# Attention and channel mix on one core: units of 448 tokens across batch ends, scores in 64x64 tiles, TensorE in traced order, weight decode with PSUM, shared staging slots

## The chip, the cores and the metric

The kernel runs on one core of one Trainium2 chip. The metric is the device time of one launch in microseconds (us). TensorE (PE) multiplies, VectorE (DVE), ScalarE (ACT) and GpSimd (POOL) do the elementwise work, and SyncE (SP) issues every DMA of this kernel.

## The reference

Sliding-window attention feeds a channel mix. Attention's arrays are float32, and there are 8 batches, 8 heads, 576 tokens and 64 columns per head.

```python
# attention, per batch and head: window of 64 keys, causal
scores = (q @ k.T) / sqrt(64)
mask = (rel >= 0) & (rel < 64)            # rel = query - key
attn = exp(where(mask, scores, -1e9) - max)
attn = attn / (attn.sum(-1) + 1e-9)
x = heads side by side(attn @ v)          # 576 x 512 for each batch

# channel mix, per batch
x_prev = x shifted down one token, zero first
xk = mu_k * x + (1 - mu_k) * x_prev
xr = mu_r * x + (1 - mu_r) * x_prev
kk = maximum(xk @ w_k, 0.0)               # 512 x 1024
out = sigmoid(xr @ w_r) * ((kk * kk) @ w_v)
```

The weights w_k, w_v and w_r arrive as float64 and are decoded to float32 on the chip, since the arithmetic of the reference is kept to float32 accuracy.

## The kernel before

**Attention.** Two heads fill the 128 partitions, so there are 32 pairs. The 576 queries of a pair are 9 blocks of 64, and three blocks are a group: 96 groups in all. For a group, `scores` issues three matmuls `s` (L149). Their weights are a tile `qbd` that holds a block's queries of both heads with zeros where one head's rows meet the other's columns, so one 128x128 matmul gives the scores of both heads against 128 keys (64 keys in a pair's first block). DVE masks and takes the minimum (`sm`, L152), ACT takes the exponent and its sum (`pr`, L155), DVE inverts the sum (`rs`, L158, L159) and POOL normalises (L161). `flip` transposes the three weights on PE (`t`, L168) and ACT copies them out (`pt`, L170). `mix_v` multiplies with the values for two groups at a time (`x`, L182: 64 columns of weights, so the tile shape on PE is 128x64), and ACT copies the result to `xT` (L187). The three steps of a group are pulled one at a time, each a stage behind the next group's scores.

**Channel mix.** A unit is 288 tokens, half a batch: 16 units. `time_mix` makes `xr` and `xk` (DVE L221 and L224, ACT L225, POOL L226), each split in two float32r parts. Every product takes three matmuls per 128 rows of contraction (`product`, L235: `m`, 128x128 weights, 288 columns): 48 for `r`, 96 for `k` and 96 for `v`, 240 a unit. Behind a product of `r` come four ACT operations and one of DVE (L247 to L253), behind one of `k` ACT, POOL, ACT, DVE (L262 to L266), behind one of `v` a DVE operation and an output DMA (L275, L276). A product accumulates in one of four PSUM buffers.

**Weight decode.** 20 chunks of 128x512 doubles (512 KB each) come through three staging buffers `wst` (L102). Five DVE operations (L107 to L113) build the float, ACT rounds it to the first float32r part (L116), POOL subtracts for the second (L117). The 20 chunks are pulled while the first batch's attention and the first units are issued.

**What sets the order.** The program pulls generators in an interleaved way: first the whole attention of batch 0 with decode in between, then per step of a unit (20 steps of 12 matmuls) one attention step and at the start one decode chunk. The instructions are then put in order on each engine by a scheduler that works with a simulated timeline, and it may move instructions of every engine, PE included, past each other as far as the data allow.

Of the kernel before, what the change touches and what calls it, by code (L numbers as in the profile page):

```python
# [23 lines left out]
NG = NB // G  # L24
# [6 lines left out]
STAGES = 3 * (NP * NG + 2)   # steps of a batch's attention  # L31
LEAD = 8             # steps by which attention is ahead of the channel mix
MIX_AT = 11          # step of a MoE unit at which the next one's mixing begins
R_BUFS = 4           # gates, which become outputs
WB = 3               # chunks of weights in flight
WC = 512             # weight columns decoded at a time
# High words of doubles as float32 values: 2**-127, and the largest float32 of 12 bits.
# [5 lines left out]
def attn_rwkv_kernel(ctx, tc, qT, kT, v2, mu_k, mu_r, w_k, w_v, w_r, out):  # L43
# [12 lines left out]
    # queries of a pair by block, the heads' apart: zero where a head's rows meet the  # L56
    # other head's columns
    qbd = [const.tile([P, NB, 2, W], F32, name=f"qbd{i}") for i in range(2)]
    nc.vector.memset(qbd[0][:, :G], 0.0)
    nc.vector.memset(qbd[0][:, G:], 0.0)  # L60
# [7 lines left out]
    mask0 = const.tile([P, W], F32, name="mask0")  # L68
    nc.gpsimd.memset(mask, 0.0)
    nc.gpsimd.memset(mask0, 0.0)  # L70
    for h in range(2):
        m = mask[h * W:(h + 1) * W]
        nc.gpsimd.affine_select(out=m, in_=m, compare_op=ALU.is_ge, fill=NEG, base=-1,
                                pattern=[[1, P]], channel_multiplier=-1)
        nc.gpsimd.affine_select(out=m, in_=m, compare_op=ALU.is_ge, fill=NEG, base=W,
                                pattern=[[-1, P]], channel_multiplier=1)
        m = mask0[h * W:(h + 1) * W]
        nc.gpsimd.affine_select(out=m, in_=m, compare_op=ALU.is_ge, fill=NEG, base=0,
                                pattern=[[-1, W]], channel_multiplier=1)

    nc.gpsimd.memset(qbd[1], 0.0)
    # the first group's weights: its first block has none for the other keys
    pr0 = const.tile([P, G, P], F32, name="pr0")
    nc.gpsimd.memset(pr0[:, 0, W:], 0.0)
# [9 lines left out]
    # A weight comes as a double: its low word and its high word. The float's bits are  # L94
    # sign and top exponent bit of the high word, its next 27 bits and 3 bits of the low
    # word; a magnitude outside float32's normal range is brought to its ends first.
    def weights():
        for dst, src in ((wr_s, w_r), (wk_s, w_k), (wv_s, w_v)):
            for c in range(0, dst.shape[3], WC):
                for i in range(dst.shape[2]):  # L100
                    st = tmp.tile([P, WC, 2], U32, name="wst", bufs=WB)
# [3 lines left out]
                    t = tmp.tile([P, WC], U32, name="wt")  # L105
                    tf = t.bitcast(F32)
                    nc.vector.tensor_scalar(t, hi, 0x7FFFFFFF, None, op0=ALU.bitwise_and)  # L107
                    nc.vector.tensor_scalar(tf, tf, HI_MIN, HI_MAX, op0=ALU.max, op1=ALU.min)  # L108
                    nc.vector.tensor_scalar(t, t, 3, 0x3FFFFFF8,  # L109
                                            op0=ALU.logical_shift_left, op1=ALU.bitwise_and)  # L110
                    nc.vector.scalar_tensor_tensor(t, hi, 0xC0000000, t,  # L111
                                                   op0=ALU.bitwise_and, op1=ALU.bitwise_or)
                    nc.vector.scalar_tensor_tensor(t, lo, 29, t,  # L113
# [7 lines left out]
    loaded = {}  # L121

    def load_pair(n, cuts=(0, NB)):
        """cuts: the blocks at which q and k are cut into transfers."""
        q = qbd[n % 2]
        k = ld.tile([P, S], F32, name="k")
        for i0, i1 in zip(cuts, cuts[1:]):
            nc.sync.dma_start(k[:, i0 * W:i1 * W], kT[n, :, i0 * W:i1 * W])
            for h in range(2):
                nc.sync.dma_start(q[h * W:(h + 1) * W, i0:i1, h, :],  # L130
                                  qT[n, h * W:(h + 1) * W, i0 * W:i1 * W].rearrange("p (i r) -> p i r", r=W))
        v = ld.tile([P, 2, 4, P], F32, name="v")
        nc.sync.dma_start(v, v2[n])
        loaded[n] = (q, k, v)

    def scores(n, g):
        q, k, _ = loaded[n]
        ps = ps_s.tile([P, G, P], F32, name="s")
        # sm = -(scaled and masked scores), nmax = their minimum
        sm = at.tile([P, G, P], F32, name="sm", bufs=3)  # L140
        nmax = at.tile([P, G], F32, name="nmax", bufs=4)
        pr = pr0 if g == 0 else at.tile([P, G, P], F32, name="pr")
        sums = at.tile([P, G], F32, name="sums", bufs=4)
        # keys of a block's window: the block before and the own one, if there are two
        nks = [W if g == 0 and j == 0 else P for j in range(G)]
        for j, nk in enumerate(nks):
            i = G * g + j
            k0 = (i + 1) * W - nk
            nc.tensor.matmul(ps[:, j, :nk], q[:, i].rearrange("p h r -> p (h r)"),  # L149
                             k[:, k0:k0 + nk], start=True, stop=True)  # L150
        for j, nk in enumerate(nks):
            nc.vector.tensor_tensor_reduce(sm[:, j, :nk], ps[:, j, :nk], mask if nk == P else mask0,  # L152
                                           scale=-SCALE, scalar=FAR, op0=ALU.add, op1=ALU.min,
                                           accum_out=nmax[:, j:j + 1])
            nc.scalar.activation(pr[:, j, :nk], sm[:, j, :nk], AF.Exp, bias=nmax[:, j:j + 1], scale=-1.0,  # L155
                                 accum_out=sums[:, j:j + 1])
# [3 lines left out]
        for j, nk in enumerate(nks):  # L160
            nc.gpsimd.tensor_scalar(pr[:, j, :nk], pr[:, j, :nk], rs[:, j:j + 1], 1.0,  # L161
                                    op0=ALU.mult, op1=ALU.mult)
        return pr

    def flip(pr):
        ps = ps_t.tile([P, G, P], F32, name="t")
        for j in range(G):
            nc.tensor.transpose(ps[:, j, :], pr[:, j, :], ident)  # L168
        pt = at.tile([P, G, P], F32, name="pt", bufs=3)
        nc.scalar.copy(pt, ps)  # L170
        return pt

    def mix_v(groups, xT):
        """Groups (pair, group, weights) together, as changing to half the columns costs."""
        ps = ps_x.tile([P, len(groups), G, W], F32, name="x")
        for e, (n, g, pt) in enumerate(groups):
            v = loaded[n][2]
            for j in range(G):
                i = G * g + j
# [117 lines left out]
    xTs = {}  # L297
# [69 lines left out]
```

## Time and profile before

| | |
|---|---|
| time, median of 3 runs | 712.29 us (709.93 to 712.74) |
| profiled execution, first to last instruction (span) | 711.3 us; the page gives no other time for it, and the median of the runs is 1.0 us above |
| instructions | 15989 |
| PE busy | 682.2 us (96%), 5856 matmul records |
| DVE, ACT, POOL busy | 415.5, 413.9, 364.9 us |
| HBM read, written | 46.14 MB, 9.44 MB |

A float32 matmul leaves two matmul records (s: 288 matmuls, 576 records; x: 576 and 1152), a float32r matmul (m) and a transpose (t) one. Records overlap, because matmuls are pipelined: the mean length of a record is not the time between two of them. That time is read from the chain of waits, where a piece "PE m L235 x744" has its length and its count. Start times are counted from the first instruction.

### The profile page before, as it was taken

The numbers are of one execution on the slowest core, as the hardware profiler recorded it, in microseconds if no ns is written. First come the engines' busy times: TensorE is split into PE (matmuls) and PEld (weight loads), VectorE is DVE, ScalarE is ACT, GpSimd is POOL, SyncE is SP. The second block draws the span as 40 slices with busy tenths as digits, with TensorE's granted clock in tenths as the row PEclk, the third lists the DMA queues.
The fourth block names the chain that finished last, engine by engine and source line by source line (L and its number), as shares of the span: only waits on it lengthen the run. The fifth ranks groups of instructions, "written<-read, shape, count | busy, mean of one in ns | idle before, by whom it ended". The sixth has DMA issues, their size and how long they took to land.

```text
span 711.3 us, 15989 instructions
## 1 busy us (share of the span) xinstructions
PE 682.2 (96%) x5856; PEld 657.9 (92%) x5856; DVE 415.5 (58%) x1326; ACT 413.9 (58%) x1397; POOL 364.9 (51%) x580
## 2 busy tenths in 40 slices
PE   6878878999999999999999999999999999999998
PEld 5766777799999999999999999999999999999998
DVE  3999999955545455465535455463645556463421
ACT  4768775663626383748566575756756475644351
POOL 4788898754335272554626355453624546252420
PEclk9999898999999999999999999999999999999999
DMA  8885666620000001221222222211323221000000
GB/s 208 237 234 152 189 178 176 166 73 26 10 34 2 34 31 64 65 89 45 85 63 72 68 64 88 73 55 44 95 66 94 67 64 48 18 1 35 26 9 34
DMA packets 59742, 56.61 MB, mean 80 GB/s; under 512 B 40592, under 2 KB 49040, under 8 KB 59664
## 3 DMA queue, kind: packets, MB, share of 16 engines
q1 hardware_dynamic: 59664, 55.59, 26.7%
q8 instruction: 46, 0.75, 0.5%
q14 instruction: 32, 0.26, 0.1%
HBM read 46.14 MB, written 9.44 MB: 78 GB/s over the span
## 4 chain that ended last, share of the span: by engine, by line
PE 80%; DVE 15%; POOL 1%; issue 1%; DMA 1%; SPq 1%; ACT 0%
PE m L235 68%; PE s L149 6%; PE x L182 4%; PE t L168 3%; DVE sm L152 2%; DVE wt L111 2%; DVE wt L107 2%; DVE wt L113 2%; DVE xm L224 1%; DVE wt L109 1%; DVE wt L108 1%; DVE rs L158 1%; POOL pr L161 1%; DMA qbd<-qT 1%; DVE d L221 1%
## 5 line engine op out<-in xcount | busy, mean ns | idle before, releaser
L235 PE MATMUL m<-ks,wv_s 128*128 128x288 f32 x1536 | 226.1, 301 | 1.0 <-ACT wv_s L116 0.9
L235 PE MATMUL m<-xk,wk_s 128*128 128x288 f32 x1536 | 221.2, 299 | 2.0 <-POOL wk_s L117 2.0
L161 POOL TENSOR_SCALAR pr<-pr,rs 128x128 f32<-128x128 f32 (+1 forms) x288 | 129.7, 467 | 173.0 <-DVE rs L159 62.4
L235 PEld LDWEIGHTS m<-ks,wv_s 128*128 128x128 f32 x1536 | 208.7, 190 | 2.5 <-ACT wv_s L116 1.3
L235 PEld LDWEIGHTS m<-xk,wk_s 128*128 128x128 f32 x1536 | 207.0, 189 | 3.6 <-POOL wk_s L117 2.2
L155 ACT ACTIVATE pr<-sm,nmax 128x128 f32<-128x128 f32 (+1 forms) x288 | 111.6, 391 | 68.0 <-DVE nmax L152 67.9
L263 POOL TENSOR_TENSOR kf<-kf 128x288 f32<-128x288 f32 x128 | 93.2, 733 | 81.1 <-ACT kf L262 80.1
L266 DVE TENSOR_TENSOR ks<-kf,ks 128x288 fp32r<-128x288 f32 x128 | 72.6, 571 | 71.5 <-ACT ks L265 71.3
L235 PE MATMUL m<-xr,wr_s 128*128 128x288 f32 x768 | 113.1, 299 | 1.0 <-POOL xr L226 1.0
L235 PEld LDWEIGHTS m<-xr,wr_s 128*128 128x128 f32 x768 | 103.5, 188 | 2.4 <-POOL xr L226 1.9
L149 PE MATMUL s<-k,qbd 128*128 128x128 f32 (+1 forms) x576 | 88.4, 294 | 15.7 <-DVE nmax L152 9.0
L149 PEld LDWEIGHTS s<-k,qbd 128*128 128x128 f32 x576 | 79.0, 205 | 19.0 <-DVE nmax L152 11.2
L226 POOL TENSOR_TENSOR xr<-xm,xr 128x288 fp32r<-128x288 f32 x64 | 56.4, 891 | 71.2 <-ACT xr L225 68.4
L152 DVE CUSTOM_DVE_ANT_0 sm<-s,mask 128x128 f32<-128x128 f32 (+1 forms) x288 | 66.7, 276 | 36.1 <-PE s L149 36.0
L262 ACT ACTIVATE kf<-m 128x288 f32<-128x288 f32 x128 | 52.2, 409 | 36.8 <-PE m L235 29.5
L224 DVE SCALAR_TENSOR_TENSOR xm<-d,muk,xT 128x288 f32<-128x288 f32 x64 | 55.2, 862 | 26.7 <-POOL xr L226 26.6
L265 ACT CAST ks<-kf 128x288 fp32r<-128x288 f32 x128 | 55.1, 431 | 24.9 <-POOL kf L263 24.5
L253 DVE SCALAR_TENSOR_TENSOR r<-th,e 128x288 f32<-128x288 f32 x64 | 34.2, 535 | 50.4 <-ACT th L251 50.1
L247 ACT ACTIVATE e<-m 128x288 f32<-128x288 f32 x64 | 26.2, 410 | 60.9 <-PE m L235 60.7
L168 PE MATMUL t<-ident,pr 128*128 128x128 f32 x288 | 55.4, 284 | 6.2 <-POOL pr L161 3.4
L275 DVE SCALAR_TENSOR_TENSOR r<-m,r 128x288 f32<-128x288 f32 x64 | 28.3, 451 | 56.4 <-PE m L235 56.4
L226 POOL TENSOR_TENSOR xk<-xm,xk 128x288 fp32r<-128x288 f32 x64 | 58.5, 933 | 5.2 <-ACT xk L225 5.2
(44 smaller groups left out, 652.7 us busy)
## 6 DMA issues: line engine op xcount, KB each, us to landing
v<-v SPq DMA_DIRECT2D x32, 512.0 KB, 3.6
outT<-r SPq DMA_DIRECT2D x64, 144.0 KB, 1.7
k<-kT SPq DMA_DIRECT2D x31, 288.0 KB, 3.1
qbd<-qT SPq DMA_DIRECT2D x62, 144.0 KB, 3.6
wst<-w_k SPq DMA_DIRECT2D x8, 512.0 KB, 4.1
wst<-w_v SPq DMA_DIRECT2D x8, 512.0 KB, 3.6
wst<-w_r SPq DMA_DIRECT2D x4, 512.0 KB, 7.6
k<-kT SPq DMA_DIRECT2D x1, 192.0 KB, 2.4
```

What stands on the lines that cost most here:

```text
L149: nc.tensor.matmul(ps[:, j, :nk], q[:, i].rearrange("p h r -> p (h r)"), k[:, k0:k0 + nk], start=True, stop=True)
L152: nc.vector.tensor_tensor_reduce(sm[:, j, :nk], ps[:, j, :nk], mask if nk == P else mask0, scale=-SCALE, scalar=FAR, op0=ALU.add, op1=ALU.min,
L155: nc.scalar.activation(pr[:, j, :nk], sm[:, j, :nk], AF.Exp, bias=nmax[:, j:j + 1], scale=-1.0, accum_out=sums[:, j:j + 1])
L161: nc.gpsimd.tensor_scalar(pr[:, j, :nk], pr[:, j, :nk], rs[:, j:j + 1], 1.0, op0=ALU.mult, op1=ALU.mult)
L168: nc.tensor.transpose(ps[:, j, :], pr[:, j, :], ident)
L224: nc.vector.scalar_tensor_tensor(xm, d, mu[:, c:c + 1], xp, op0=ALU.mult, op1=ALU.add)
L226: nc.gpsimd.tensor_sub(xs[:, 1, c], xm, xs[:, 0, c].bitcast(F32))
L235: nc.tensor.matmul(ps, w[:, a, c, col * P:(col + 1) * P], x(c, e), start=(i == 0), stop=(i == last))
L262: nc.scalar.activation(kf, ps, AF.Relu)
L263: nc.gpsimd.tensor_mul(kf, kf, kf)
L265: nc.scalar.copy(ks[:, 0], kf)
L266: nc.vector.tensor_sub(ks[:, 1], kf, ks[:, 0].bitcast(F32))
```

## The change

- **Units.** `UNITS` replaces 16 units of 288 tokens by 11: 256, 320 and nine of 448. A unit may begin in one batch and end in the next (`parts`), so `time_mix` works piece by piece, and `v_units` issues one output DMA per piece. The count of `m` falls from 3840 to 2640, and the columns that they stream stay 240 x 4608.
- **Scores.** `qbd` with its zeros is gone; `q` is loaded as it lies, in one transfer a pair. The 9 blocks of two pairs are dealt to three rounds of six (`slots`): 48 rounds instead of 96 groups. A round issues 12 matmuls `s`, each of 64 rows by 64 columns of weights against 128 keys. The head picks the 64 rows and the PSUM tile, the block's half the 64 columns. Each round's masked scores are written back to PSUM in place, and `soft` runs once per head. A block's first-block mask is now 128 wide, like the others.
- **Order on PE.** Every matmul and transpose goes through `tc.keep_in_program_order`: PE runs them as they are traced. In `attention`, a round's `s` and the `x` of the round two before are traced next to each other; the flips of the two heads follow one step apart. The first 24 steps of attention stand ahead of the first unit, and `by` spreads the rest so that a batch is done by the step at which its time mix begins.
- **Decode.** The `and` with 0x7FFFFFFF becomes ACT's absolute value. Four DVE operations are left; the second writes a PSUM tile (`wp`, a buffer of the products' pool), which the third rewrites and the fourth reads.
- **Staging slots.** Weight chunks are staged in the eight slots that later hold `ks`; `wt`, `d`, `xm`, `th` and `kf` share five slots of one tag.

```diff
-TH = S // 2          # tokens of a MoE unit
+UNITS = (4, 5) + (7,) * 9
+TU = max(UNITS) * W
+USTEPS = 20
+TB = 5
...
+    def matmul(*args, **kw):
+        tc.keep_in_program_order(nc.tensor.matmul(*args, **kw))
...
-                    st = tmp.tile([P, WC, 2], U32, name="wst", bufs=WB)
+                    st = act.tile([P, WC, 2], U32, name="wst", tag="ks", bufs=8)
...
-                    nc.vector.tensor_scalar(t, hi, 0x7FFFFFFF, None, op0=ALU.bitwise_and)
+                    pt = ps_m.tile([P, WC], U32, name="wp", tag="m")
+                    tf = tmp.tile([P, WC], F32, name="wt", tag="tmp", bufs=TB)
+                    nc.scalar.activation(tf, hi.bitcast(F32), AF.Abs)
                     nc.vector.tensor_scalar(tf, tf, HI_MIN, HI_MAX, op0=ALU.max, op1=ALU.min)
-                    nc.vector.tensor_scalar(t, t, 3, 0x3FFFFFF8,
+                    nc.vector.tensor_scalar(pt, tf.bitcast(U32), 3, 0x3FFFFFF8,
                                             op0=ALU.logical_shift_left, op1=ALU.bitwise_and)
-                    nc.vector.scalar_tensor_tensor(t, hi, 0xC0000000, t,
+                    nc.vector.scalar_tensor_tensor(pt, hi, 0xC0000000, pt,
                                                    op0=ALU.bitwise_and, op1=ALU.bitwise_or)
-                    nc.vector.scalar_tensor_tensor(t, lo, 29, t,
+                    nc.vector.scalar_tensor_tensor(tf.bitcast(U32), lo, 29, pt,
                                                    op0=ALU.logical_shift_right, op1=ALU.bitwise_or)
...
-        q = qbd[n % 2]
+        q = ld.tile([P, S], F32, name="q")
...
+    def slots(n, g):
+        if g == 1:
+            return [((n, 6), (n, 7)), ((n, 8), (n + 1, 8)), ((n + 1, 6), (n + 1, 7))]
+        n += g // 2
+        return [((n, i), (n, i + 1)) for i in range(0, 2 * G, 2)]
+
+    def scores(sl):
+        ps = [ps_s.tile([P, G, P], F32, name="s") for _ in range(2)]
+        for e, halves in enumerate(sl):
+            for j, (n, i) in enumerate(halves):
+                q, k, _ = loaded[n]
+                k0 = max(i - 1, 0) * W
+                for h in range(2):
+                    hr = slice(h * W, (h + 1) * W)
+                    matmul(ps[h][j * W:(j + 1) * W, e, :], q[hr, i * W:(i + 1) * W],
+                                     k[hr, k0:k0 + P], start=True, stop=True)
+        return [soft(ps[h], sl) for h in range(2)]
...
-            nc.tensor.matmul(ps[:, j, :nk], q[:, i].rearrange("p h r -> p (h r)"),
-                             k[:, k0:k0 + nk], start=True, stop=True)
...
+                a1[t] = scores(slots(n, g))
+            if t >= 2:
+                n, g = items[t - 2]
+                mix_v(slots(n, g), a2.pop(t - 2))
+            yield
+            for h in range(2):
+                if t - 1 in a1:
+                    a2.setdefault(t - 1, []).append(flip(a1[t - 1][h]))
+                yield
...
+    per = STEPS * ROUNDS
+    ran = per + 2 * STEPS
+    for i in range(ran):
         run(ats, 1)
-        if i >= 5 and i % 3 == 0:
+        if i >= 2 and i % 2 == 0:
             run(wl, 1)
...
+    by = [(0, ran)]
+    for b in range(1, B):
+        u = min(u for u in range(len(UNITS)) if parts(u)[-1][0] >= b)
+        by.append(((u - 1) * USTEPS + MIX_AT, per * (b + 1) + 2 * STEPS))
```

Two places in the order of the instructions show what this does. On PE, in the middle of the program, before (`m` with `ks,wv_s` is a product of `v`, with `xr,wr_s` one of `r`; s, t and x are scores, transposes and values):

```order
L235 MATMUL m<-xr,wr_s 128x288 x12
L182 MATMUL x<-pt,v 64x64 x12
L235 MATMUL m<-xr,wr_s 128x288 x12
L149 MATMUL s<-k,qbd_83 128x128 x3
L235 MATMUL m<-xk,wk_s 128x288 x12
L168 MATMUL t<-ident,pr_114 128x128 x3
```

On PE in the changed kernel, in the third unit's products of `v` (L60 and L63 are the lines of the two wrappers):

```order
L60 MATMUL m<-ks,wv_s 128x448 x12
L60 MATMUL s<-k,q 64x128 x12
L60 MATMUL x<-pt,v 64x64 x12
L60 MATMUL m<-ks,wv_s 128x448 x12
L63 MATMUL t<-ident,pr 128x128 x3
L60 MATMUL m<-ks,wv_s 128x448 x12
L63 MATMUL t<-ident,pr 128x128 x3
```

A round's twelve score matmuls now stand directly ahead of twelve value matmuls, where three scores stood between products; each head's three transposes stand between two products.

On DVE near the start, where the first weights are decoded, before (`wt<-wst` reads the staged double, `sm` is a masked score; the chunk's L107 stands a few rows ahead):

```order
L152 ISA sm,nmax<-s,mask 128x128
L152 ISA nmax 128x1
L108 TENSOR_SCALAR wt<-wt 128x512
L158 TENSOR_SCALAR rs<-sums 128x3
L109 TENSOR_SCALAR wt<-wt 128x512
L159 RECIPROCAL rs<-rs 128x3
L111 SCALAR_TENSOR_TENSOR wt<-wst,wt 128x512
L221 TENSOR_TENSOR d<-xT 128x288
L113 SCALAR_TENSOR_TENSOR wt<-wst,wt 128x512
```

On DVE at the same stage of the changed kernel (`wp` is the PSUM tile):

```order
L111 TENSOR_SCALAR wt<-wt 128x512
L163 ISA s,nmax<-s,mask 128x128
L163 ISA nmax 128x1
L112 TENSOR_SCALAR wp<-wt 128x512
L163 ISA s,nmax<-s,mask 128x128
L163 ISA nmax 128x1
L114 SCALAR_TENSOR_TENSOR wp<-wst,wp 128x512
L111 TENSOR_SCALAR wt<-wt 128x512
L116 SCALAR_TENSOR_TENSOR wt<-wst,wp 128x512
```

A chunk now takes four DVE rows, and two chunks overlap among the masked scores.

More of the change, by code (lines that the diff above doesn't have):

```diff
@@ L141, in scores, with soft @@
+    def soft(ps, sl):
         nmax = at.tile([P, G], F32, name="nmax", bufs=4)
-        pr = pr0 if g == 0 else at.tile([P, G, P], F32, name="pr")
+        pr = at.tile([P, G, P], F32, name="pr", bufs=3)
         sums = at.tile([P, G], F32, name="sums", bufs=4)
[L145 to L149, printed above, removed]
-                             k[:, k0:k0 + nk], start=True, stop=True)
@@ L166, in flip @@
         ps = ps_t.tile([P, G, P], F32, name="t")
-        for j in range(G):
-            nc.tensor.transpose(ps[:, j, :], pr[:, j, :], ident)
+        for e in range(G):
+            transpose(ps[:, e, :], pr[:, e, :], ident)
         pt = at.tile([P, G, P], F32, name="pt", bufs=3)
@@ L320, in steps @@
         def steps():
[L321 to L325 removed]
+            yield from r_units(xr, gate, n)
+            yield from k_units(xk, k2, n)
+            run(wl)
+            yield from v_units(u, k2, gate, n)
+        for i, _ in enumerate(steps()):
             run(wl, 1)
             done += 1
[L328 to L331 removed]
+            for (d0, a0), (d1, a1) in zip(by, by[1:]):
+                if d0 < done <= d1:
+                    due = a0 + -(-(a1 - a0) * (done - d0) // (d1 - d0))
+                    run(ats, due - ran)
+                    ran = due
+            if i == MIX_AT and u + 1 < len(UNITS):
+                assert all(b in ready for b, _, _ in parts(u + 1))
                 mixed = new_mixed()
[L333 removed]
+                nxt = time_mix(u + 1, *mixed)
             run(nxt, 1)
```

218 lines of the change are left out of this document (103 added, 115 removed).

## The prediction

> **What bounds the kernel now.** I read the page first, then the busy time by stretch, then the chain of waits. The page has PE at 96% of the span and full from the eighth slice on; DVE is full ahead of that:
>
> ```profile
> span 711.3 us, 15989 instructions
> PE   6878878999999999999999999999999999999998
> DVE  3999999955545455465535455463645556463421
> ```
>
> The stretches (us busy and instructions of PE, PEld, DVE, ACT, POOL, then the granted clock, the DMA share and GB/s) were cut where the chain changes hands:
>
> ```profile
> 12.70:141.70 129.00, 110.16 (x1008) 94.96 (x1008) 122.38 (x449) 91.17 (x343) 106.61 (x151) 0.93 0.67 193
> 145.90:708.20 562.30, 562.28 (x4789) 554.42 (x4787) 286.09 (x836) 314.34 (x1023) 248.87 (x400) 1.00 0.17 51
> 708.20:711.30 3.10, 0.00 (x0) 0.00 (x0) 0.46 (x1) 0.00 (x0) 0.00 (x0) 1.00 0.13 48
> ```
>
> So there are two stages. Up to 141.7 us DVE is busy 122.4 of 129 us, with the weight decode; from 145.9 to 708.2 us PE never stops and no other engine passes 56%. The first stage costs what PE leaves undone in it, the second is the time between matmuls times their number. The chain of waits gives that time (start, length, engine, line, count):
>
> ```profile
> 145.94 98.47 PE m L235 x744
> 314.89 0.67 PE s L149 x6
> 317.16 0.33 PE t L168 x3
> 324.85 0.85 PE x L182 x24
> 325.70 1.78 PE m L235 x12
> 328.14 1.59 PE m L235 x12
> 144.57 0.50 PE x L182 x12
> 145.07 0.86 PE s L149 x6
> ```
>
> Per record: m 98.47/744 = 132.4 ns, s 0.67/6 = 112 ns, t 0.33/3 = 110 ns. A visit to x of 24 records costs 0.85 us, and 0.19 more in the m behind it (1.78 against 1.59): 1.04. One of 12 costs 0.50 + 0.19 (s 0.86 against 0.67) = 0.69. Twelve records are therefore 0.35, or 29 ns each, and entering plus leaving the 128x64 tile shape costs 0.34: 0.15 in, 0.19 out. These prices close on the second stage, whose counts are
>
> ```profile
> L235 PE MATMUL m<-ks,wv_s 128*128 128x288 f32 x1440 | 207.8, 299 | 0.0
> L235 PE MATMUL m<-xk,wk_s 128*128 128x288 f32 x1440 | 203.7, 298 | 0.0
> L235 PE MATMUL m<-xr,wr_s 128*128 128x288 f32 x720 | 104.6, 299 | 0.0
> L149 PE MATMUL s<-k,qbd 128*128 128x128 f32 (+1 forms) x307 | 43.1, 275 | 0.0
> L168 PE MATMUL t<-ident,pr 128*128 128x128 f32 x174 | 30.7, 272 | 0.0
> L182 PE MATMUL x<-pt,v 128*64 128x64 f32 x708 | 28.0, 226 | 0.0
> ```
>
> 3600 x 0.1324 + 307 x 0.112 + 174 x 0.110 + 708 x 0.029 + some 30 visits x 0.34 = 476.6 + 34.4 + 19.1 + 20.5 + 10.2 = 560.8, against 562.3 measured. PE's time is its list of matmuls.
>
> **Wider units.** The m fall from 3840 to 2640 and stream the same columns, so only what a matmul costs beside its columns is saved, and that part no row gives alone. Two rows bound it: 128 columns of t take 110 ns, and two records of x side by side, 64 columns each, 58 ns. That is 0.81 ns a column and 6 ns fixed. m takes 0.46 ns a column, about half, so I halve the slope: 0.405 x 288 + 6 = 123 ns, 9 less than the 132.4 seen. If those 9 ns are paid per matmul, 448 columns take 197 ns, 320 take 145 and 256 take 119; a unit has 240, so m becomes 240 x (119 + 145 + 9 x 197) = 489 us against 3840 x 0.1324 = 508: 19 us less. If they grow with the columns, nothing is saved (508); if they vanish at 448, it is 188 ns and about 469. I take 489, the middle, as a fixed gap is the plain reading of a price above the slope.
>
> The Trainium skill's page "TensorE: Matmul & The Clock Gate", section "Wait — 56ns, not 53.3ns?", puts back-to-back warm matmuls at N/2.4 + about 2.5 ns, which is 122.5 ns for 288; the trace's 132.4 disagrees by 10 ns. By that rule 448 columns would take 189 ns and m 467 us.
>
> **Scores in 64x64 tiles.** A round now has 12 matmuls, 24 records, where two groups had 12 records. In x, two column halves run side by side: 29 ns a record, where t's price for half its columns would be 55. If all four quarters run so, a round is 6 records long, 0.67 us; if only the column halves do, 1.34; if none, 2.7. No row shows two row halves side by side. I take 0.67, since the heads write different PSUM tiles and x shows independent tiles in the other direction. Entering the 64x64 shape costs 0.15 as entering x does: 0.82 a round against 1.34.
>
> The skill's page "TensorEngine Tiling (Array Packing)", section "Key Properties", speaks for and against: different tiles load and multiply in parallel, and a change of tiling mode drains the engine. By it a round drains three times where a visit to x drains twice; x's 0.15 and 0.19 agree.
>
> x stays at 1.04 a visit and t at 0.66 a round. With s, 48 rounds cost 48 x (0.82 + 1.04 + 0.66) = 121 us, and PE's whole list is 489 + 121 = 610.
>
> **Decode and start.** The work that DVE had in the first stage, by line (busy, mean ns):
>
> ```profile
> L152 DVE CUSTOM_DVE_ANT_0 sm<-s,mask 128x128 f32<-128x128 f32 (+1 forms) x117 | 27.1, 271 | 4.5 <-PE s L149 4.5
> L111 DVE SCALAR_TENSOR_TENSOR wt<-wst,wt 128x512 uint32<-128x512 uint32 x20 | 19.3, 963 | 0.2
> L113 DVE SCALAR_TENSOR_TENSOR wt<-wst,wt 128x512 uint32<-128x512 uint32 x20 | 17.0, 850 | 0.1
> L107 DVE TENSOR_SCALAR wt<-wst 128x512 uint32<-128x512 uint32 x20 | 14.5, 724 | 2.1 <-POOL wk_s L117 1.5 <-POOL wr_s L117 0.6
> L109 DVE TENSOR_SCALAR wt<-wt 128x512 uint32<-128x512 uint32 x20 | 11.9, 596 | 0.1
> L108 DVE TENSOR_SCALAR wt<-wt 128x512 f32<-128x512 f32 x20 | 10.7, 534 | 0.1
> ```
>
> Decode is 73.4 us of the 122.4; the other 49 go with 117 `sm`. The change moves L107's 14.5 us to ACT, which gets 20 operations like its cast of the same size:
>
> ```profile
> L116 ACT CAST wk_s<-wt x8: 614/618/632, 47.2 to 94.2; 128x512 fp32r<-128x512 f32 x8
> L111 DVE SCALAR_TENSOR_TENSOR wt<-wst,wt x20: 673/756/1835, 20.3 to 139.5; 128x512 uint32<-128x512 uint32 x20
> L113 DVE SCALAR_TENSOR_TENSOR wt<-wst,wt x20: 653/692/1759, 21.4 to 140.3; 128x512 uint32<-128x512 uint32 x20
> ```
>
> That is 12.4 us in a stretch where ACT is busy 91 of 129, so hidden. What PSUM operands do to the other four no row shows: at today's means they are 58.9 us; if the slow cases go (minimum 673, maximum 1835) and L111 and L113 fall to their medians 756 and 692, 51.6. I take 53. With the last chunk DVE will have done only about 60 `sm`, half of 117, so of the 49 us some 26. That makes 79 us. But the new DVE order has 11 chunks early, then 27 `sm` with no decode between them, where DVE waits for rounds that run one behind the other; I add 12. The first stage then ends at 12.7 + 79 + 12 = 104 us, not 141.7 (90 to 130). The DMAs are a bound of the same size: weights (20 x 512 KB) and nine pairs (1.1 MB each) are 20 MB, 104 us at the stage's 193 GB/s; the 130 takes that in.
>
> By then PE can have done 11 s, 9 t and 9 x of the rounds and 144 m of 256 columns: 11 x 0.82 + 9 x 0.66 + 9 x 1.04 + 17 = 41 us. Behind it stand 610 - 41 = 569.
>
> **PE's fixed order.** From 145.9 us PE had no idle time, with an order that the scheduler was free to choose. Now products queue behind any t, x or s that is late. x stands a product and a round's s (2.4 + 0.8 us) behind the last t, and needs ACT's copy; the last product of k has 21 m (4.1 us) as cover for ACT, POOL, ACT, DVE:
>
> ```profile
> L170 ACT COPY pt<-t 128x384 f32<-128x384 f32 x58 | 27.7, 477 | 8.0 <-PE t L168 7.9
> L262 ACT ACTIVATE kf<-m 128x288 f32<-128x288 f32 x128 | 52.2, 409 | 36.8 <-PE m L235 29.5
> L263 POOL TENSOR_TENSOR kf<-kf 128x288 f32<-128x288 f32 x128 | 93.2, 733 | 81.1 <-ACT kf L262 80.1
> L265 ACT CAST ks<-kf 128x288 fp32r<-128x288 f32 x128 | 55.1, 431 | 24.9 <-POOL kf L263 24.5
> L266 DVE TENSOR_TENSOR ks<-kf,ks 128x288 fp32r<-128x288 f32 x128 | 72.6, 571 | 71.5 <-ACT ks L265 71.3
> ```
>
> The chain is 2.1 us at 288, at most 3.3 at 448. Both covers hold unless an engine's queue holds the step up by a microsecond, so I charge 4 us in all, bounds 0 and 45. Sharing five slots is in the same 4: a late `kf` would hold the same chain. Edits at nothing: the pieces at batch ends add DVE operations and output DMAs, the 64 wider mask columns some DVE time, both under a DVE that is 51% busy; `q` in one transfer has half the issues; deeper staging of weights only starts DMAs earlier.
>
> **The sum.** 104 + 569 + 4 + the tail of 3.1 = 680 us of span, against 711.3. The profiled span is 1.0 below the median of the runs, so 681; I say 680.
>
> **Rivals.**
> - *The fixed part grows with the columns.* For it: no row separates the two. m stays at 508, 19 more: 699. Chance 0.15.
> - *The extra 9 ns vanish at 448 columns.* For it: the slope of t and x. m is 469, 20 less: 660. This is also the way of the skill's N/2.4 rule above. Chance 0.15.
> - *The 64x64 tiles do not do what they say.* If row halves take turns, a round is 1.34 + 0.15, 0.67 more, x 48 = 32: 712, no change. Against it: x's halves. Chance 0.08.
> - *PE's own order stalls it* (slower). Its place is each round's t, x and s in the middle of the run, while m that are ready stand behind. There are 37 rounds after the start; from 0.9 us lost in each, 33 us, the whole gain is gone, and at 1.1 it is 41: 721. For it: ACT now serves 37 rounds there instead of the 26 of before (307 records of s), in front of longer operations. Against it: ACT is 56% busy there. Chance 0.12.
>
> **How the numbers follow.** The forecast has 0.50 (665 to 697 by the bounds of the start and small stalls). Faster by over 0.5% (3.6 us, about what a measurement of this kernel can tell from no change) are the forecast and the first two rivals: 0.80. Within it lies the third: 0.08. Slower: 0.12. The range goes from 655, below the vanishing gap with few stalls, to 714, over the third rival; what is left out is most of the slower case and a little below.
>
> **What would show it.** In the profile of the changed kernel: the chain's long m pieces at 197 ns a matmul in a pure stretch (206: first rival; 188: second); s of a round at about 0.7 us and not 1.4; the last decode operation near 104 us; PE idle under 5 us between then and the end. A PE that waits for ACT's `pt` or POOL's `pr` in every round would make the prediction wrong.

## The result, and the profile after

The changed kernel takes 755.3 us (median, 753.87 to 756.33) where the kernel before took 712.51 on the same chip (709.93 to 713.12): the ratio is 1.0602, 95% interval 1.0579 to 1.0626. It is 6% slower, where 4.5% faster was forecast. The profiled execution has a span of 753.3 us, 42 more than before.

The page of the changed kernel, span, busy times and three of the 40-slice rows:

```profile
span 753.3 us, 14304 instructions
PE 666.0 (88%) x5232; PEld 589.8 (78%) x5232; DVE 407.5 (54%) x1236; ACT 413.0 (55%) x1217; POOL 326.9 (43%) x499
PE   3457747898999899989999999989997999999998
DVE  4985754737545834763484374374349335528121
PEclk9999977899999999999999999999999999999999
```

PE is less busy than before in total, so its list did get shorter. But its row is low for the first eight slices, and after that single 8s and a 7 recur where the kernel before had nothing but 9s. DVE's row no longer has the wall of 9s at the start. Busy time by stretch (us busy and instructions of PE, PEld, DVE, ACT, POOL; then PE's granted clock, DMA share, GB/s):

```profile
0.00:60.00 60.00, 26.91 (x267) 18.60 (x267) 43.53 (x141) 33.57 (x106) 31.45 (x60) 1.00 0.67 235
60.00:140.00 80.00, 51.10 (x455) 43.64 (x456) 49.48 (x150) 44.44 (x145) 36.78 (x58) 0.83 0.26 84
140.00:172.00 32.00, 32.00 (x343) 30.74 (x342) 16.01 (x66) 21.37 (x74) 15.12 (x28) 1.00 0.26 83
172.00:240.00 68.00, 64.20 (x582) 58.24 (x581) 36.39 (x125) 42.79 (x136) 34.93 (x56) 0.95 0.24 77
240.00:400.00 160.00, 152.21 (x1284) 132.59 (x1285) 96.71 (x319) 94.47 (x292) 73.66 (x116) 0.98 0.23 74
400.00:520.00 120.00, 115.09 (x842) 103.05 (x832) 63.54 (x183) 67.00 (x188) 53.47 (x79) 0.99 0.18 59
520.00:623.20 103.20, 98.13 (x855) 86.11 (x853) 49.77 (x178) 62.15 (x189) 39.40 (x70) 1.00 0.18 58
623.20:750.00 126.80, 126.37 (x624) 116.82 (x624) 51.80 (x77) 47.18 (x90) 42.15 (x37) 1.00 0.06 21
```

Two things went wrong, and both show here. From 60 to 140 us no engine is near full (DVE 49.5 of 80, PE 51.1 of 80, DMA 26%), the sign of a chain in which engines wait for each other; PE's clock is at 0.83 on top. And from 172 to 623 us PE is idle about a twentieth of every stretch (3.8 + 7.8 + 4.9 + 5.1 = 21.6 us), with a clock of 0.95 to 0.99 in three of them. Two stretches are clean: 140 to 172 us, where rounds of attention run but no time mix, and the last, with no attention left.

**PE's list came out almost as forecast.** From the chain of waits: the clean piece at the end, and a round in the middle of a unit (start, length, engine, line, count):

```profile
623.19 126.40 PE m L60 x624
```

```profile
264.59 2.43 PE m L60 x12
267.02 0.82 PE s L60 x24
267.83 0.85 PE x L60 x24
268.68 2.63 PE m L60 x12
271.31 0.33 PE t L63 x3
```

126.40/624 = 202.6 ns for `m` at 448 columns. A round of scores costs 0.82 us, a visit to x 0.85 and 0.2 in the `m` behind it, three `t` 0.33: the three prices of the prediction. With 132.4 ns at 288 columns, `m` is 6.0 ns + 0.439 ns a column, so 118 at 256, 146 at 320, and 240 x (118 + 146 + 9 x 202.6) = 501 us. With 121 for the rounds the list is 622 us. Before, it was 662: 562 from 145.9 us on, and ahead of that 240 `m`, 269 `s`, 114 `t` and 444 `x` in 37 visits, 100 by the prediction's prices. That is 40 us less, instead of the 52 that the forecast's 610 would have saved.

**The start.** The first product of v begins at 127.7 us. By then PE has done what the prediction listed for its 104 us (11 rounds of s, 9 of t, 9 of x, 144 m: 41 us), so 87 us were lost there. In the kernel before, at 145.9 us, PE had done 100 us and lost 46. The four DVE operations of a decode, in the first 140 us:

```profile
L112 DVE TENSOR_SCALAR wp<-wt 128x512 uint32<-128x512 uint32 x20 | 14.0, 700 | 0.3
L114 DVE SCALAR_TENSOR_TENSOR wp<-wst,wp 128x512 uint32<-128x512 uint32 x20 | 13.9, 697 | 0.1
L116 DVE SCALAR_TENSOR_TENSOR wt<-wst,wp 128x512 uint32<-128x512 uint32 x20 | 13.6, 680 | 0.2
L111 DVE TENSOR_SCALAR wt<-wt 128x512 f32<-128x512 f32 x20 | 10.2, 511 | 7.9 <-ACT wt L110 7.6
```

They sum to 51.7 us; 53 was forecast. Decode is as cheap as it was meant to be, and still ends late: the chunks' last steps start at 18 to 47 us for the first eleven and at 83 to 128 us for the other nine. Loading is not what holds the next four: chunks 12 to 15 had landed by 38.8 us. From 47 to 79 us DVE works on the last rounds of batch 0, one behind the other, and ACT's first step for chunk 12, at 78.9 us, stands behind its operations for the first unit's first product. The chain of waits in the second part, one chunk long (pieces under 0.2 us left out):

```profile
104.52 0.56 ACT wt L110
105.10 0.43 DVE wt L111
105.69 0.48 issue
106.33 0.67 DVE wp L114
107.02 0.70 DVE wt L116
107.74 0.63 ACT wv_s L119
108.44 0.25 POOL wv_s L120
108.69 0.98 issue
109.67 0.62 POOL kf L295
110.32 0.41 ACT ks L297
110.72 0.36 ACT pr L166 x2
111.08 0.59 ACT wt L110
```

A chunk goes through ACT, DVE, ACT and POOL, then POOL and ACT square and split a product of `k` of the first unit, and behind that ACT begins the next chunk, 6.6 us after the one before. The last steps of the nine late chunks start 5.5 us apart on average, those of the last four 6.2 to 6.6.

**The gaps later.** On ACT at 249 us (start, length, operation, idle time before it and its releaser):

```profile
249.42 0.56 ACT L258 CAST xr<-xm 128x448 fp32r<-128x448 f32 x1 [3.20 <-DVE xm L254]
249.89 0.36 ACT L166 ACTIVATE pr<-s,nmax 128x128 f32<-128x128 f32 x1
...
250.59 0.47 ACT L180 COPY pt<-t 128x384 f32<-128x384 f32 x1
```

and on DVE and on PE around it:

```profile
245.51 0.14 DVE L163 DVE_READ_ACCUMULATOR2_ANT nmax<- 128x1 f32 x1
245.51 2.61 DVE L252 TENSOR_TENSOR d<-xT 128x128 f32<-128x128 f32 x2
248.05 0.61 DVE L298 TENSOR_TENSOR ks<-kf,ks 128x448 fp32r<-128x448 f32 x1
248.58 0.80 DVE L254 SCALAR_TENSOR_TENSOR xm<-d,mur,xT 128x128 f32<-128x128 f32 x2
```

```profile
248.72 0.68 PE L60 MATMUL m<-ks,wv_s 128*128 128x448 f32 x2 [0.38 <-DVE ks L298]
251.16 0.52 PE L63 MATMUL t<-ident,pr 128*128 128x128 f32 x3 [1.77 <-issue]
```

The next unit, the fourth, lies across a batch end, so its time mix comes in two pieces (128 and 320 columns). DVE works through both; ACT's cast of `xr` waits 3.20 us for it, and the exponents and the copy to `pt` that a round needs stand behind that cast: the exponent at 249.89 us had its scores' minimum from DVE at 245.65. The copy to `pt` ends at 251.06, and only then is the one PSUM tile of `t` free again; PE starts the next `t` at 251.16, having waited 1.77 us, while the `m` behind it follow without a gap. Such gaps of 0.4 to 2.9 us, at `t`, `s` or `x`, stand near 182 to 188, 249 to 257, 318 to 325, 399, 450, 503 to 507 and 573 to 578 us, each time while the next unit's time mix runs or just behind it. Five of these seven units cross a batch end; with the short waits of `m` beside them they hold about 17 of the 21.6 us. The third and the seventh unit (182 to 188 and 450 us) lie in one batch, their time mix is in one piece of 448 columns, and they still hold 4.5: two pieces are not needed for a gap. In four of the seven places the clock also drops to half, for 3.4 us at a time:

```profile
246.00:262.00 16.00, 12.81 (x95) 10.31 (x94) 14.61 (x44) 8.37 (x30) 10.09 (x14) 0.89 0.15 49
```

0.89 over 16 us is about 3.4 us at half. The Trainium skill's page "TensorE: Matmul & The Clock Gate", section "What's actually happening", says that the clock is gated to half after an idle window of about 3.4 us, in a window that runs freely. The length agrees; but in this stretch PE is idle for 3.2 us in all, in pieces of at most 1.77. Idle time alone doesn't decide it either: near 573 to 578 us PE is idle for 5.1 us and the clock stays up.

**The balance**: -40 (list) + 41 (start, 87 against 46) + 41 (behind the start: 26 idle, the 21.6 above and the rest ahead of 140 us; some 12 from the half clock; 3 unassigned) = 42, the difference of the two spans.

### The profile page after: what moved, and what is told of

Same layout as the page of the kernel before. It is cut to its first block, busy times and chain, and to the rows that moved or that the text cites. A ratio compares the mean times of both kernels' runs of the same rounds, so it can differ in the third digit from the quotient of the medians.

```text
span 753.3 us, 14304 instructions
## 1 busy us (share of the span) xinstructions
PE 666.0 (88%) x5232; PEld 589.8 (78%) x5232; DVE 407.5 (54%) x1236; ACT 413.0 (55%) x1217; POOL 326.9 (43%) x499
## 4 chain that ended last, share of the span: by engine, by line
PE 63%; DVE 22%; ACT 6%; POOL 3%; issue 3%; DMA 1%; SPq 1%; POOLq 0%; ACTq 0%; DVEq 0%
PE m L60 53%; DVE xm L254 7%; PE s L60 4%; PE x L60 4%; DVE d L252 4%; PE t L63 3%; DVE s L163 3%; ACT pr L166 2%; DVE ks L298 2%; POOL kf L295 2%; DVE wp L114 2%; DVE wt L116 1%; DVE rs L169 1%; DMA wst<-w_r 1%; DVE wt L111 1%
## 5 line engine op out<-in xcount | busy, mean ns | idle before, releaser
L60 PE MATMUL m<-xk,wk_s 128*128 128x448 f32 (+2 forms) x1056 | 217.6, 360 | 18.0 <-ACT kf L294 13.0
L60 PE MATMUL m<-ks,wv_s 128*128 128x448 f32 (+2 forms) x1056 | 224.8, 366 | 6.3 <-ACT ks L297 3.2
L60 PEld LDWEIGHTS m<-xk,wk_s 128*128 128x128 f32 x1056 | 188.3, 192 | 32.2 <-ACT kf L294 13.8
L60 PEld LDWEIGHTS m<-ks,wv_s 128*128 128x128 f32 x1056 | 191.6, 195 | 22.9 <-DVE ks L298 5.5
L172 POOL TENSOR_SCALAR pr<-pr,rs 128x128 f32<-128x128 f32 x288 | 113.6, 411 | 206.4 <-DVE rs L170 118.5
L166 ACT ACTIVATE pr<-s,nmax 128x128 f32<-128x128 f32 x288 | 106.3, 370 | 109.6 <-DVE nmax L163 85.8
L295 POOL TENSOR_TENSOR kf<-kf 128x448 f32<-128x448 f32 (+2 forms) x88 | 81.6, 928 | 116.3 <-ACT kf L294 116.3
L163 DVE CUSTOM_DVE_ANT_0 s<-s,mask 128x128 f32<-128x128 f32 x288 | 82.7, 301 | 72.2 <-ACT pr L166 56.3
L298 DVE TENSOR_TENSOR ks<-kf,ks 128x448 fp32r<-128x448 f32 (+2 forms) x88 | 57.2, 650 | 107.0 <-ACT ks L297 107.0
L60 PE MATMUL m<-xr,wr_s 128*128 128x448 f32 (+2 forms) x528 | 107.9, 358 | 2.0 <-ACT th L282 2.0
L60 PEld LDWEIGHTS m<-xr,wr_s 128*128 128x128 f32 x528 | 93.6, 191 | 8.5 <-ACT th L282 2.2
L60 PE MATMUL s<-k,q 64*64 64x128 f32 x1152 | 56.0, 306 | 29.6 <-ACT pr L166 25.0
L63 PE MATMUL t<-ident,pr 128*128 128x128 f32 x288 | 54.5, 303 | 26.9 <-ACT pt L180 15.6
L60 PEld LDWEIGHTS s<-k,q 64*64 64x64 f32 x1152 | 38.9, 148 | 47.5 <-ACT pr L166 31.3
L63 PEld LDWEIGHTS t<-ident,pr 128*128 128x128 f32 x288 | 39.0, 154 | 37.7 <-issue 22.1
L166 ACT ACTIVATION_READ_ACCUMULATOR pr<-s,nmax 128x1 f32 x288 | 57.1, 198 | 0.0
L60 PEld LDWEIGHTS x<-pt,v 128*64 128x64 f32 x1152 | 41.9, 151 | 10.6 <-issue 9.1
```

What stands on the lines that cost most here:

```text
L60: tc.keep_in_program_order(nc.tensor.matmul(*args, **kw))
L63: tc.keep_in_program_order(nc.tensor.transpose(*args))
L163: nc.vector.tensor_tensor_reduce(ps[:, e], ps[:, e], mask0 if sl[e][0][1] == 0 else mask, scale=-SCALE, scalar=FAR, op0=ALU.add, op1=ALU.m ...
L166: nc.scalar.activation(pr[:, e], ps[:, e], AF.Exp, bias=nmax[:, e:e + 1], scale=-1.0, accum_out=sums[:, e:e + 1])
L172: nc.gpsimd.tensor_scalar(pr[:, e], pr[:, e], rs[:, e:e + 1], 1.0, op0=ALU.mult, op1=ALU.mult)
L295: nc.gpsimd.tensor_mul(kf, kf, kf)
```

## The experiments

Five causes were left: TensorE's fixed order (the prediction's slower rival, below called the order), the decode's place, the wider units, and the two kinds of shared slots. Each run below was timed against the kernel before on the same chip. "Own staging" is three slots for weight chunks and two for `wt`, apart from the others. Where a kernel changes an earlier one, its diff is given on top of that.

**e1_unpinned**: the changed kernel, with the scheduler free to order PE.

```diff
-        tc.keep_in_program_order(nc.tensor.matmul(*args, **kw))
+        nc.tensor.matmul(*args, **kw)
-        tc.keep_in_program_order(nc.tensor.transpose(*args))
+        nc.tensor.transpose(*args)
```

> The changed kernel without the fixed order on PE; all else stays. Since the first chunk of decode, PE has lost 88 us until the decode's end (before: 48) and some 39 us behind it (27 idle, 12 at half clock). Theory A (the fixed order costs both losses): 675 to 695 us. Theory B (the start is lost because chunks 12 to 20 of the decode come one at a time beside the first unit, from shared slots and their place in the program, whatever PE's order): only the later losses go, 710 to 725. Theory C (the later stalls come from time mix in two pieces at batch ends, on DVE): 735 to 755.

756.43 us, 1.062 (1.0592 to 1.0648): no gain, where theory A had 675 to 695 us; theory C, the nearest, had 735 to 755. PE fills its idle time at the start (30 us instead of 54 before the first product of v), but that product comes at 143 us instead of 127.7. Idle time behind it falls from 26 to 12 us. So the order by itself does not explain the loss in this kernel; what the next run shows is that this is not because the order is harmless.

**e2_before_pinned**: the kernel before, with its PE instructions kept in traced order, and nothing else.

```diff
-            nc.tensor.transpose(ps[:, j, :], pr[:, j, :], ident)
+            transpose(ps[:, j, :], pr[:, j, :], ident)
...
-                nc.tensor.matmul(ps, w[:, a, c, col * P:(col + 1) * P], x(c, e),
+                matmul(ps, w[:, a, c, col * P:(col + 1) * P], x(c, e),
```

> The kernel before with PE held to its traced order, nothing else changed. Theory A: it loses as the changed kernel does, 745 to 790 us against 712. Theory B: it loses little at the start, since its chunks have slots of their own and stand in the attention of batch 0: 712 to 725. Theory C: no change, as no unit crosses a batch end: 712 to 720.

750.72 us, 1.0545 (1.0512 to 1.0578): 39 us lost. The same stretch, first of this kernel, then of the kernel before:

```profile
52.00:100.00 48.00, 20.52 (x132) 17.05 (x133) 42.96 (x118) 20.31 (x67) 30.68 (x34) 0.50 0.48 147
```

```profile
52.00:100.00 48.00, 41.89 (x377) 36.47 (x375) 46.30 (x156) 36.20 (x132) 40.29 (x57) 0.89 0.60 179
```

PE does a third of the instructions, all of them at half clock: with a fixed order it can't take up the first units' `m` while a round's chain is under way, falls idle again and again, and the clock stays down. Behind the first product of v (124.7 us) only 7.7 us are idle. In this kernel the order costs mainly at the start, not in each round.

**e4_decode_early**: the changed kernel, with all 20 chunks ahead of the first unit.

```diff
-        if i >= 2 and i % 2 == 0:
+        if i >= 2:
```

> The changed kernel with one chunk of decode pulled at every attention step ahead of the first unit, so that all 20 stand there, in place of 11 there and 9 beside the first unit. Theory B: the start's extra loss goes, 715 to 730 us against 755. Theory A: under 10 us are gained, 745 to 755. Theory C says nothing of the start: 745 to 755.

735.64 us, 1.0342 (1.0311 to 1.0373): 20 less, between the ranges of theories A and B. The last chunk's last step now starts at 72 us, yet the first product of v only at 112.6, with 46 us of idle time ahead of it. Its clock row:

```profile
PEclk9755699999999999999999999999999999999999
```

Decode stops being the last thing; the rounds, one behind the other with DVE full of decode, are next, and the idle PE runs them at half clock from 26 to 84 us.

**e5_units_256_320**: the changed kernel with units that end with the batches.

```diff
-UNITS = (4, 5) + (7,) * 9
+UNITS = (4, 5) * 8
```

> The changed kernel with 16 units of 256 and 320 tokens in turn, so that no unit crosses a batch end; as many matmuls m as before. By the matmul prices m costs about 6 us more than in the changed kernel. Theory C: the later stalls go (27 idle and 12 at half clock), 720 to 735 us. Theories A and B: the stalls stay, 755 to 770.

733.01 us, 1.0294 (1.0277 to 1.0311): 22 less, although `m` as a whole costs 508 us again instead of 501. The start is unchanged (first product of v at 126.6). Behind it:

```profile
126.60:400.00 273.40, 266.49 (x2696) 255.21 (x2698) 158.40 (x531) 175.80 (x594) 137.72 (x234) 0.99 0.22 72
400.00:728.00 328.00, 324.98 (x3071) 315.96 (x3060) 175.02 (x510) 188.23 (x601) 147.80 (x238) 1.00 0.16 51
```

Idle time is 9.9 us instead of 26, and from 141 us to the last matmul there is no half clock. PE's order is still fixed. So the units of 448 tokens cost about 22 + 7 = 29 us. This run takes away three things at once: the width, the crossing of batch ends, and with them the steps at which rounds are traced. The traces tell a little more. With PE free (e1) every gap over 0.25 us behind 152 us stands in the time mix of the fourth, fifth, eighth or ninth unit, which cross a batch end, and none in that of the third, which doesn't; with the order fixed the third has 3.8 us too.

**e6_256_320_early**: e5 and e4 together.

> Both edits that gained so far: units of 256 and 320 and all 20 chunks of decode pulled ahead of the first unit. They act in different stages, the one behind 130 us and the other ahead of it, so if the two losses are separate the gains add: 755.3 - 22 - 20 = 713 us (709 to 718). If both are one loss, 725 to 733.

715.0 us, 1.005 (1.0035 to 1.0065). The two gains add (755 - 20 - 22 = 713): the start and the wide units are separate costs.

**e7_own_staging**: e5 with slots of their own for chunks (three instead of eight shared) and `wt` (two instead of five shared).

```diff
-                    st = act.tile([P, WC, 2], U32, name="wst", tag="ks", bufs=8)
+                    st = tmp.tile([P, WC, 2], U32, name="wst", bufs=3)
...
-                    tf = tmp.tile([P, WC], F32, name="wt", tag="tmp", bufs=TB)
+                    tf = tmp.tile([P, WC], F32, name="wt", bufs=2)
```

> Units of 256 and 320, and weights staged in three slots of their own and decoded in two of their own, as in the kernel before, instead of the eight shared ones and the five shared ones. Theory D (eight staging slots let 11 chunks of decode run ahead of the attention on DVE, so PE has nothing to do, and the shared slots then tie the last 9 chunks to the products of the first unit): the first product of v comes at about 105 us and not 127, 712 to 720 us against 733. If the slots don't matter: 730 to 735.

717.66 us, 1.0085 (1.007 to 1.01): 15 less than e5, nearly all of it ahead of the first product of v (112.2 us instead of 126.6, where 105 was expected). The hole behind the 11th chunk stays: chunk 12 has its `wt` from ACT at 56 us, but its `wp` starts only at 76.4, right behind DVE's last `xm` of the first unit's time mix.

**e8_own_all**: e7, and own slots for `d` (2), `xm` (3), `th` (2) and `kf` (2).

```diff
-            d = tmp.tile([P, TU], F32, name="d", tag="tmp", bufs=TB)
+            d = tmp.tile([P, TU], F32, name="d", bufs=2)
...
-            kf = tmp.tile([P, TU], F32, name="kf", tag="tmp", bufs=TB)[:, :n]
+            kf = tmp.tile([P, TU], F32, name="kf", bufs=2)[:, :n]
```

> As the run with own staging slots, and d, xm, th and kf in buffers of their own too (2, 3, 2, 2). If sharing five slots among them held the chain behind a product of k, 5 to 15 us less than with own staging alone; if it is only the staging, the same within 3 us.

723.77 us, 1.0177 (1.016 to 1.0194): 6 slower than e7, which neither expectation had. Sharing the five slots among these four is no cost; parted, there are gaps of 0.5 us at `t` and 1.0 at `m` in nearly every pair of units.

**e9_own_staging_free**: e7 with e1's free order.

> As the run with own staging slots, and PE's order free. Theory A (the fixed order keeps PE idle in the start): 10 to 25 us less than with the fixed order. If the free order buys its gain with more changes of tile shape between scores and values, as in the first run of this kind, the same within 4 us.

691.96 us (690.82 to 694.46), 0.9729 (0.9708 to 0.9751): 26 less than e7, and faster than both kernels, by 2.7% than the one before. Its page and first stretches:

```profile
span 689.1 us, 17092 instructions
PE   4879899999999999999999999999999999999998
```

```profile
0.00:96.00 96.00, 74.94 (x701) 60.27 (x701) 82.27 (x288) 73.97 (x249) 62.70 (x114) 0.98 0.64 215
96.00:400.00 304.00, 301.89 (x3061) 290.93 (x3061) 180.66 (x582) 195.26 (x654) 154.06 (x262) 1.00 0.23 72
```

DVE is at 82 of 96 us again, PE at 75, and the first product of v is at 96.0 us. Decode's last step starts at 96 us too, with no hole behind the 11th chunk (55.0 us, then 58.1): about where the prediction had it (104), once nothing ties it.

**e10_256_320_free**: e5 with e1's free order, the slots shared as in the change.

> Units of 256 and 320, shared slots as in the changed kernel, PE's order free. With 448 tokens and shared slots the free order gained nothing (756 against 755), with own staging slots and 256/320 it gained 26 (692 against 718). If it is the shared staging that eats the free order's gain: 728 to 736, as with the fixed order. If it is the wide units: 700 to 712, the fixed order's 733 less the same 26.

726.82 us, 1.0214 (1.0197 to 1.0231): only 6 less than e5, and 35 more than e9. The free order is worth 26 us with own staging and 6 without. In the chain of waits of this kernel the last five chunks stand one behind the other, each with its load:

```profile
118.57 5.50 DMA wst<-w_v
124.07 0.02 issue
124.09 0.03 ACT wt L110
```

Their loads start at 86, 96, 105, 119 and 131 us. Eight slots let the first chunks in at once, and they stand ahead of attention on DVE: the fifth round's scores start at 39.8 us here and at 30.6 in e9. Chunks 12 to 15 have landed by 38.4 us and are taken up by ACT only from 70.5 us on (52.6 in e9), so it is not the load that they wait for. The last five get a slot only in turn with `ks`, and their loads stand on SyncE's one queue behind those of k and v, which wait for PE's rounds (42 us for `s` alone by the waits of that queue).

**e11_free_early**: e9 with e4's early decode.

> The fastest run so far (own staging, 256/320, free order) with a chunk of decode pulled at every attention step, all 20 ahead of the first unit. If the decode's end at 97.6 us is still what the first product of v waits for, as there, v begins some 10 us earlier: 680 to 687. If the earlier decode only holds up the attention on DVE: 692 to 702.

698.83 us, 0.9815 (0.9801 to 0.983): 7 slower than e9. Decode ends nine microseconds sooner (88.5 instead of 97.6) and the first product of v is later (103.7 instead of 96.0): chunks that come too early hold up attention on DVE. What helped the fixed order (e4) harms the free one.

**e13_tight_448_free** and **e14_tight_256_320_free**: free order and own staging with 448-token units, for which the staging had to shrink (two slots for chunks, one for `wt`, two for v instead of three), and the same with units of 256 and 320. The pair was to show the wide units without the other two costs.

```diff
-                    st = act.tile([P, WC, 2], U32, name="wst", tag="ks", bufs=8)
+                    st = tmp.tile([P, WC, 2], U32, name="wst", bufs=2)
-                    tf = tmp.tile([P, WC], F32, name="wt", tag="tmp", bufs=TB)
+                    tf = tmp.tile([P, WC], F32, name="wt", bufs=1)
-        v = ld.tile([P, 2, 4, P], F32, name="v", bufs=3)
+        v = ld.tile([P, 2, 4, P], F32, name="v", bufs=2)
```

> Units of 256, 320 and nine of 448 again, with staging slots apart from the others as far as the memory allows (two for wst, one for wt, two for v), PE's order free. Its pair is the same kernel with units of 256 and 320. By the matmul prices m is some 6 us cheaper at 448. If a free order hides the time mix in two pieces, it is 0 to 8 us faster than its pair. If the batch ends stall DVE's queue whatever PE's order, 8 to 25 us slower than its pair.

> The pair of the run before: two slots for wst, one for wt, two for v, free order, units of 256 and 320. Against the fastest run so far, which has three, two and three, the tighter staging should slow the decode: 695 to 710 us.

760.99 us, 1.0685 (1.0665 to 1.0705), and 727.63 us, 1.0221 (1.0201 to 1.024). The second was expected far lower: the tighter staging alone costs 36 us against e9, with the first product of v at 145.5 us. But that start is the same in both, so the pair still tells what it was for. The stretch behind it, of e13 and then of e14:

```profile
145.50:400.00 254.50, 249.42 (x1934) 220.03 (x1935) 139.86 (x424) 145.77 (x428) 114.92 (x167) 0.97 0.20 64
```

```profile
145.50:400.00 254.50, 252.19 (x2445) 244.54 (x2446) 146.72 (x428) 156.93 (x503) 123.19 (x195) 0.99 0.20 61
```

Wide units cost 33 us with a free order too, more than the 8 to 25 expected: 9.8 us of idle time behind the start against 4.2, all of it in the time mixes of four units that cross a batch end, 27 us at half clock against 3.4 (some 12 lost), and 248 changes of tile shape against 180. How the rest of the 33 splits, no run tells apart.

The whole in one table (us):

| units | slots of chunks and `wt` | order fixed | order free |
|---|---|---|---|
| 448 | shared | 755.3 (the change) | 756.4 (e1) |
| 256, 320 | shared | 733.0 (e5) | 726.8 (e10) |
| 256, 320 | own | 717.7 (e7) | 692.0 (e9) |
| 288, the kernel before | own | 750.7 (e2) | 712.5 |

## Why the prediction was wrong

The sum was 104 + 569 + 4 + 3 = 680. Measured in the same terms it is 127.7 + 581 + 42 + 3 = 753: 24 us at the start, 12 on the list, 38 in stalls. Each of the three ended inside the bounds that the prediction gave it, all near the far end (127.7 of 130 for the start, 42 of 45 for the stalls, 501 of 508 for `m`); the range to 714 left no room for all of them at once.

- **Scores in 64x64 tiles: right.** 0.82 us a round, as taken. All four quarters run side by side, and rival 3 falls.
- **Wider units: mis-sized.** "If those 9 ns are paid per matmul, 448 columns take 197 ns." It is 202.6, nearer the rival in which the gap grows with the columns (206). A matmul costs 6 ns beside its columns, so 1200 fewer of them save 7 us, not 19. Halving the slope of t and x was the mistake: it gave 0.405 ns a column, and `m` has 0.439, with 6 ns beside the columns and no further 9.
- **Decode and start: the DVE sum held, the end did not.** The four operations took 51.7 us (53 forecast). The step that failed is "I add 12" for an order in which the chunks come in two lots: between the 11th and the 12th lie 36 us, and the last nine go one after the other beside the first unit's products, 5.5 us each on average. I took DVE's work for the bound where the place of the chunks, their slots and the fixed order made a chain. e4 (20 us), e7 (15) and e9 against e10 (35) show that place and slots set it.
- **PE's fixed order: charged 4 us, bounds 0 and 45.** The order costs 39 us in the kernel before (e2), 26 with 256/320 and own staging (e7, e9), and 6 or nothing with shared slots (e5, e10; the change, e1), since there decode ends late either way (128 us fixed, 141 to 145 free). The rival that had it slower (721) had the sign and half of the place. In the changed kernel PE does stand at `t`, `s` and `x` of rounds in the middle of the run with `m` behind them, but in seven places, not in each of 37 rounds, and without the wide units (e5) the fixed order loses only 10 us of idle time there. Most of what the order costs by itself is at the start: 16 of the 26 us between e7 and e9 lie ahead of the first product of v.
- **Edits at nothing: wrong, and the largest miss behind the start.** "The pieces at batch ends add DVE operations ... under a DVE that is 51% busy." The average was no cover. The operations of a time mix come together, longer at 448 columns and in two pieces at a batch end, and a round's exponents and copies stand behind them. With the half clock that follows this is most of the 41 us behind the start; units of 256 and 320 give it back (e5: 22 us net; e13 against e14: 33). The prediction named the pieces alone; the third unit shows that one piece of 448 columns can do it too, and no run parts the two.
- **Shared slots.** Sharing five among `d`, `xm`, `th` and `kf` was rightly charged at nothing (e8). "Deeper staging of weights only starts DMAs earlier" was wrong, as far as e7 goes, which takes the chunks and `wt` out together: the first eight, started earlier, stand ahead of attention on DVE, and the last five wait for their turn. Which of the two slots counts for more, no run shows.

Rivals of an `m` price alone could not go past 699. What was missing was one in which several instructions in order on DVE and ACT delay a round and PE may take nothing else: the forecast's "both covers hold unless an engine's queue holds the step up by a microsecond" named the condition and gave it no weight. Not settled: why DVE's operations stretch so far in the time mix (below), the split between width and crossing and of e13's 33 us, and what `wp` costs, which shares the products' four PSUM buffers in every run of the changed kernel.

## What to carry to other kernels

A busy share is no cover for work that comes in a lump: look at what stands in front of the lump and behind it on each in-order queue, and who waits for that. Fixing the order of the engine that bounds the kernel takes away its only way to fill a chain's gaps; it is safe where no chain is longer than the work traced in front of it, which is least true at the start. And prefetch depth can act as a priority: with eight slots the weight chunks came ahead of attention on the engine that the two share, and the late chunks came later.

## What the runs showed of the hardware

- A float32r matmul of 128x128 weights with a weight load each costs 6.0 ns + 0.439 ns a column (132.4 ns at 288, 202.6 at 448). The rule that the prediction set beside it (the Trainium skill, "TensorE: Matmul & The Clock Gate", section "Wait — 56ns, not 53.3ns?") gives 189 ns at 448, 13 fewer than measured.
- A round of 24 records of 64x64 weights against 128 keys takes 0.82 us, of which 0.67 are left behind the prediction's 0.15 for the change of shape: 28 ns a record, where one record of 128 columns by itself takes 110 (`t`).
- Operations of the time mix on DVE are longer beside POOL's. In the changed kernel 70 `xm` with no POOL operation beside them take 461 ns on average, 58 that lie mostly beside one take 1019; in the kernel before, where all have 288 columns, it is 508 (30) and 870 (92). The first pair mixes pieces of 64 to 448 columns, but it holds at one width too: 673 (7) and 1239 (16) at 448. No run took POOL's part away, so this is a coincidence in time and no proof of the cause.
